# Linear attention, dense gated layer and routed experts on one core: the order of the first loads, of the route's parts and of TensorE around the last route

## The chip, the cores and the metric

The kernel runs on one core of one Trainium2 chip. The metric is the device time of one execution in microseconds (us). A core has TensorE (PE, with its weight loads listed apart as PEld), VectorE (DVE), ScalarE (ACT), GpSimd (POOL) and SyncE (SP), each with an instruction order of its own, which are tied together by semaphores. The order of the instructions on each engine is set when the kernel is built, by a scheduler that starts from the order of the code and from the dependencies that the code states.

## What is computed

Three layers in a row, in float32. Shapes: 8 sequences of 576 tokens, 8 heads of 64; 4608 tokens of 512; a dense gated layer with 1536 hidden channels; 8 experts with 1024 hidden channels.

```python
kv  = einsum('bhsd,bhse->bhde', k, v)                 # per sequence and head
out = einsum('bhsd,bhde->bhse', q, kv)
x   = out / sqrt(mean(out*out, -1) + 1e-6) * g_norm   # -> [4608, 512]
x   = (silu(x @ w_gate) * (x @ w_val)) @ w_out        # dense layer
# experts: only tokens with x @ w_skip > 0; the others are passed through
e   = argmax(x @ w_gate2);  p = softmax(x @ w_gate2)[e]
out = x + p * (relu(x @ w1[e]) @ w2[e])
```

## The kernel before

The tokens are worked on in 12 chunks of 384. Heads come in 4 pairs. For a pair of a sequence, the keys and values lie in DRAM as rows of 5 tokens (1280 numbers, keys then values), 116 rows to a pair (`PK`), and `attn_load` fetches them as 112 and 4 rows into a tile kv (`spread`), and the transposed queries into a tile qt. `attn_unit` does the attention of a pair: `attn_kv` sums keys times values on TensorE (kvp, line 211) and copies the two 64x64 blocks into a block-diagonal matrix kvbd (ScalarE line 213, VectorE line 214); then queries times that matrix (op, line 227), the sum of squares (sq on ScalarE, ms on VectorE, lines 233 to 236), the root on GpSimd (y, line 238), and the normalised tile xn on VectorE (line 240). `make_xT` transposes xn on TensorE (xtps, line 262) and splits it into a high and a low part.

All matrix products of the layers run on numbers that are split into two parts, as three products. The dense layer's weights come as bits of float64 and are brought into this form by the kernel itself: `load_w` fetches 1 MB (raw, line 315), and for each of its two halves ScalarE scales (line 284), VectorE does three steps (cv, cv, raw: lines 286, 287, 290), ScalarE rounds the high part (w, line 296) and GpSimd subtracts (line 254). There are 18 such tiles (12 of the gate and value weights, 6 of the output weights), all converted during chunk 0 and kept afterwards. For each chunk and each f of 12, `moe1_g` does 24 matmuls (gv, line 346), silu on ScalarE, the multiply on VectorE (line 353) and the split of the hidden tile hT, and `moe1_out` does 9 matmuls (acc, line 367) for the f before. The attention of the next chunk is put between them.

When a chunk is done, its rows x are copied out, and during the next chunk VectorE works out 9 logits for each of its tokens (line 400). `chunk_route` then picks the expert (lines 432 to 440), keeps a running count of the tokens per expert (cum, line 443), and lets TensorE rank the tokens (rp, lines 446 and 447); VectorE makes row numbers of that (lines 448 to 452), and GpSimd scatters the rows into one list per expert in DRAM (line 454). After the chunk before the last but one `rank_experts` orders the experts by size, and in the last chunk `early_base` fixes where the first batch ends. The last chunk's logits are done on TensorE instead (`logits_pe`: transposes ltp, line 411, and products lps, line 416), with a route of its own behind it.

The experts are worked on in 9 batches. Batch 0 is the first 256 rows of the largest expert, which are there before the last chunk is routed; it runs around the last chunk's route: `moe2_h` (hp, line 633) and `moe2_out` (yacc, line 721) for each of 8 f. Batch 1 is the rest of that expert and needs the last scatter: its rows xe are loaded by SP (line 601) and transposed on TensorE (xtp, line 618). Batches 2 to 8 are the other experts.

Loads go out on SP's queue in the order of SP's instructions. A load whose tile's buffer is still in use waits on SP, and all behind it with it. Tiles called kv have two buffers, those with the tag w 18.

`after(a, b)` in the code orders instruction a behind b for the scheduler alone, if both are on the same engine; it adds no semaphore.

Of the kernel before, what the change touches and what calls it, by code (L numbers as in the profile page):

```python
# [16 lines left out]
P = 128  # L17
# [12 lines left out]
def attention_moe_moe_kernel(  # L30
# [98 lines left out]
    def attn_qt_load(c, pr):
        if c == 0:  # L130

            t = wp.tile([P, T], F32, tag="w", name="qt0")
        else:
            t = p1.tile([P, T + P], F32, tag="qt", name="qt")
        src = qT_d[pr, :, c * T:(c + 1) * T]
        if c % 3 == 1:
            cut = S - T
            nc.gpsimd.memset(t[:, cut:cut + P], 0.0)
            nc.sync.dma_start(t[:, 0:cut], src[:, 0:cut])
            nc.sync.dma_start(t[:, cut + P:], src[:, cut:])  # L140
        else:
            nc.sync.dma_start(t[:, 0:T], src)
        qt[c, pr] = t

    def attn_load(c, pr):
        if c % 3 != 2:
            b = 2 * (c // 3) + c % 3
# [191 lines left out]
    def moe1_g(c, f):  # L339
# [13 lines left out]
        nc.vector.tensor_tensor(s, ps[1], s, op=ALU.mult)  # L353
# [70 lines left out]
    def chunk_route(c):  # L424
        lg = lgt.pop(c)
        wd = wdesc.rearrange("p (o e) -> p o e", o=1).to_broadcast([P, R, E])
        eb = (elast if c == NCH - 1 else ebase).rearrange("p (o e) -> p o e", o=1).to_broadcast([P, R, E])
# [19 lines left out]
        nc.tensor.matmul(rp, onesb, ca[:, 0:R, :], start=False, stop=True)  # L447
        nc.vector.tensor_tensor(oh, rp, eb, op=ALU.add)
# [176 lines left out]
    def moe2_h(b, f):  # L625
# [142 lines left out]
    for c in range(NCH):  # L768
        for f in range(NF):
# [23 lines left out]
            if c > 0:  # L793
# [39 lines left out]
    chunk_route(NCH - 1)  # L833
    load_xe(1)
# [22 lines left out]
    load_ranks(ORDER[1:])  # L857
    for b, (r, _, n, nt) in enumerate(BATCH):
# [18 lines left out]
        for f in range(NF2):  # L877
# [9 lines left out]
            moe2_h(b, f)  # L887
# [132 lines left out]
```

## Time and profile before

| | before |
|---|---|
| runs, median (lowest to highest of 3) | 1309.68 us (1309.29 to 1310.69) |
| profiled execution, time | 1305.69 us |
| profiled execution, span of its instructions | 1304.0 us |
| busy in the span: PE, PEld | 1266.1 us (97%), 1180.2 us (91%) |
| DVE, ACT, POOL | 639.3 us (49%), 373.5 us (29%), 510.6 us (39%) |
| keys and values, loads of 112 rows | 32 of 560.0 KB |
| weights of the dense layer, loads | 17 of 1024.0 KB, 2 of 512.0 KB |

The profile is of one execution, whose own time stands beside its span. Busy time is the time in which an engine had an instruction under way; a share is that of the whole span, so it is a mean over stages which differ. A pause of TensorE is read from the brackets of its timeline.

### The profile page before, as it was taken

What the parts mean: (1) busy time and instruction counts of PE and PEld (TensorE: products, weight loads), DVE (VectorE), ACT (ScalarE), POOL (GpSimd) and SP (SyncE); (2) the same over time, 40 slices, a digit from 0 to 9 for tenths busy, and PEclk for the clock granted to TensorE, in tenths of its full rate; (3) what the DMA queues carried; (4) which work ended last, traced back from release to release, by engine and by line L of the source; (5) the groups of instructions that cost most, each with busy time, mean ns of one, the idle gap of its engine ahead of it and who ended that gap; (6) DMA issues with size and microseconds to landing.
All of it is one profiled execution on the core that took longest, in us unless ns stands there. A gap on an engine that the chain in (4) does not pass through costs nothing.

```text
span 1304.0 us, 18975 instructions
## 1 busy us (share of the span) xinstructions
PE 1266.1 (97%) x7239; PEld 1180.2 (91%) x7239; DVE 639.3 (49%) x1487; ACT 373.5 (29%) x773; POOL 510.6 (39%) x545
## 2 busy tenths in 40 slices
PE   5998999999999999999999999999999989999997
PEld 5987999999999999999999999999988978899996
DVE  5896817237164371542815418146283243544662
ACT  3664112122121221211212112121122433344441
POOL 4674323233322332223323223223346443566662
PEclk9999999999999999999999999999999999999999
DMA  9663702021120111202102021110121343555631
GB/s 299 234 220 142 229 20 74 25 68 43 39 66 1 44 55 38 73 26 63 37 7 86 8 62 49 31 51 7 51 91 36 131 149 117 170 171 165 218 121 33
DMA packets 43205, 115.68 MB, mean 89 GB/s; under 512 B 8498, under 2 KB 16690, under 8 KB 40928
## 3 DMA queue, kind: packets, MB, share of 16 engines
q1 hardware_dynamic: 31888, 95.78, 22.7%
q0 software_dynamic: 6912, 9.82, 2.2%
q10 hardware_dynamic: 4304, 8.78, 2.1%
q8 instruction: 59, 0.97, 0.3%
q14 instruction: 42, 0.34, 0.1%
HBM read 88.70 MB, written 30.80 MB: 92 GB/s over the span
## 4 chain that ended last, share of the span: by engine, by line
PE 85%; DVE 5%; DMA 4%; POOL 3%; issue 2%; ACT 1%; SPq 0%; DVEq 0%; ACTq 0%; POOLq 0%
PE gv L346 42%; PE acc L367 21%; PE hp L633 7%; PE yacc L721 4%; PE tacc L687 3%; PE kvp L211 3%; PE op L227 2%; DVE dump L400 2%; PE xtps L262 1%; DMA kv<-in_kv_dram 1%; DMA xe<-xs_dram 1%; POOL v L254 1%; DMA raw<-in_w_dram 1%; DVE ex L585 1%; POOL w L254 1%
## 5 line engine op out<-in xcount | busy, mean ns | idle before, releaser
L346 PE MATMUL gv<-xT,w 128*128 128x384 f32 x3456 | 654.7, 339 | 3.8 <-ACT w L296 2.9
L346 PEld LDWEIGHTS gv<-xT,w 128*128 128x128 f32 x3456 | 602.1, 188 | 18.3 <-ACT w L296 4.2
L367 PE MATMUL acc<-w,hT 128*128 128x512 f32 x1296 | 333.3, 397 | 5.0 <-ACT hT L355 4.0
L254 POOL TENSOR_TENSOR hT<-s,hT 128x384 fp32r<-128x384 f32 x144 | 161.6, 1122 | 403.8 <-ACT hT L355 403.3
L367 PEld LDWEIGHTS acc<-w,hT 128*128 128x128 f32 x1296 | 239.3, 188 | 49.3 <-ACT hT L355 5.6
L400 DVE CUSTOM_DVE_ANT_0 dump<-st,w9b 128x512 bf16<-128x512 f32 x297 | 234.4, 789 | 7.0
L353 DVE TENSOR_TENSOR s<-gv,s 128x384 f32<-128x384 f32 x144 | 80.1, 556 | 253.0 <-PE gv L346 186.1
L254 POOL TENSOR_TENSOR v<-rawv,v 128x512 fp32r<-128x512 f32 x102 | 133.6, 1335 | 49.9 <-ACT v L567 49.7
L352 ACT ACTIVATE s<-gv 128x384 f32<-128x384 f32 x144 | 70.6, 490 | 260.4 <-PE gv L346 251.2
L355 ACT ACTIVATE hT<-s 128x384 fp32r<-128x384 f32 x144 | 75.5, 524 | 242.5 <-DVE s L353 241.1
L633 PE MATMUL hp<-xU,v 128*128 128x256 f32 (+7 forms) x768 | 125.8, 308 | 1.6 <-DVE xU L623 1.4
L633 PEld LDWEIGHTS hp<-xU,v 128*128 128x128 f32 x768 | 113.8, 189 | 4.7 <-DVE xU L623 1.7
L238 POOL TENSOR_TENSOR y<-ms,mhalf 128x6 f32<-128x6 f32 x48 | 68.2, 1422 | 109.7 <-DVE ms L236 107.8
L235 DVE TENSOR_REDUCE ms<-sq 128x6 f32<-128x384 f32 x48 | 26.4, 550 | 105.7 <-ACT sq L233 105.7
L567 ACT ACTIVATE v<-rawv 128x512 fp32r<-128x512 f32 x128 | 73.0, 623 | 1.9 <-DMA rawv<-in_v_dram 1.9
L721 PE MATMUL yacc<-v,h2T 128*128 128x512 f32 (+3 forms) x288 | 73.3, 397 | 0.0
L642 DVE SCALAR_TENSOR_TENSOR h2T<-hp,h2T 128x256 fp32r<-128x256 f32 (+7 forms) x64 | 30.5, 479 | 82.3 <-ACT h2T L641 81.1
L721 PEld LDWEIGHTS yacc<-v,h2T 128*128 128x128 f32 (+3 forms) x288 | 50.6, 181 | 11.2
L687 PE MATMUL tacc<-h2T,v 128*128 128x318 f32 (+3 forms) x384 | 58.1, 302 | 2.1 <-ACT h2T L641 2.1
L641 ACT ACTIVATE h2T<-hp 128x256 fp32r<-128x256 f32 (+7 forms) x64 | 27.2, 428 | 104.7 <-PE hp L633 92.1
L254 POOL TENSOR_TENSOR w<-raw,w 128x512 fp32r<-128x512 f32 x34 | 44.7, 1318 | 30.4 <-ACT w L296 29.5
L687 PEld LDWEIGHTS tacc<-h2T,v 128*128 128x128 f32 x384 | 53.8, 189 | 2.9 <-ACT h2T L641 2.8
(131 smaller groups left out, 875.8 us busy)
## 6 DMA issues: line engine op xcount, KB each, us to landing
rawv<-in_v_dram SPq DMA_DIRECT2D x64, 512.0 KB
kv<-in_kv_dram SPq DMA_DIRECT2D x32, 560.0 KB
raw<-in_w_dram SPq DMA_DIRECT2D x17, 1024.0 KB
out_dram<-st SPq DMA_DIRECT2D x36, 256.0 KB
xs_dram<-zrow ACTq DMA_DIRECT2D x8, 781.5 KB
qt<-in_qT_dram SPq DMA_DIRECT2D x32, 192.0 KB
qt<-in_qT_dram SPq DMA_DIRECT2D x32, 96.0 KB
w9b<-in_w_dram ACTq DMA_DIRECT2D x3, 768.0 KB
```

Of the source, the lines that this page charges most:

```text
L238: nc.gpsimd.tensor_tensor(y, ms, mhalf[:, 0:G], op=ALU.pow)
L254: return eng.tensor_tensor(lo, raw, hi.bitcast(F32), op=ALU.subtract)
L346: nc.tensor.matmul(pt, w1t[f][:, wi, i, kk, :], xT[c, kk][:, xi, :], start=(n == 0), stop=(n == 3 * NK - 1))
L352: step["silu"] = nc.scalar.activation(s, ps[0], AF.Silu)
L353: nc.vector.tensor_tensor(s, ps[1], s, op=ALU.mult)
L355: nc.scalar.activation(h[:, 0, :], s, AF.Copy)
L367: nc.tensor.matmul(acc[c, r], hT[c, f][:, hi, r * P:(r + 1) * P], w[:, wi, f % 2, :], start=(f == 0 and n == 0), stop=(f == NF - 1 and n = ...
L400: nc.vector.tensor_tensor_reduce(out=dump, in0=xrow[c, r][:, 0:DM], in1=w9b[m // 3][:, m % 3, :], op0=ALU.mult, op1=ALU.add, scale=1.0, sc ...
L567: after(nc.scalar.activation(w[:, 0, s], raw[:, s], AF.Copy), behind)
L633: nc.tensor.matmul(pt, w[:, wi, kk, cs], xT["m", b, kk][:, xi, :], start=(i == 0), stop=(i == 3 * NK - 1))
L687: nc.tensor.matmul(acc["m", b, d], w[:, wi, f % 2, d * P:(d + 1) * P], h[:, hi, :], start=(f == 0 and n == 0), stop=(f == NF2 - 1 and n == 2),
L721: ins = nc.tensor.matmul(acc["m", b, t][0:q], h[:, hi, t * q:(t + 1) * q], w[:, wi, f % 2, :], start=(f == 0 and n == 0), stop=(f == NF2 - ...
```

## The change

Six things are done.

1. In the start the keys and values and the queries of a pair share a tile (kvq) from the pool of 18 buffers, one for each of the four pairs, so no pair waits for the buffer of another. `attn_load_first` issues the keys and values, and the queries follow in the same tile.
2. Keys and values are loaded as 128 rows (the last 12 belong to the next pair and are not used), by one DMA, in the start and in all later chunks.
3. The order of the code in the start is new: the third pair's load goes ahead of the first weights, and the next chunk's first loads and the second weights are ordered behind named instructions (`behind`).
4. `chunk_route` is cut in two: `route_rows`, with the row numbers and the scatter, is put one f later, and `rank_experts` or `early_base` two f later, each behind the multiply of that f (`step["gv"]`) on VectorE.
5. The load of batch 0's rows goes with `early_base`.
6. In batch 0 the hp matmuls of f = 1, 2, 3 and of f from 4 on are ordered on TensorE behind the second transpose of the last chunk's rows, behind the last lps (f = 2 and 3) and behind rp; the yacc matmuls of f = 0 behind the last lps, later ones behind rp.

The diff, cut to its core:

```diff
+    kv_rows = kv_d.rearrange("b q p s r c -> (b q p) s r c")
+    def attn_kv_load(c, pr, t, behind=None):
+        if c % 3 != 2:
+            b = 2 * (c // 3) + c % 3
+            row = (b * NPR + pr) * PK
+            n = min(P, B * NPR * PK - row)
+            for lo, hi in spread(n):
+                after(nc.sync.dma_start(t[lo:hi], kv_rows[row + lo:row + hi]), behind)
+            kvt[c, pr] = t
...
-    def attn_load(c, pr):
+    def attn_load(c, pr, behind=None):
         if c % 3 != 2:
-            t = p2.tile([P, 2, NR, P], F32, tag="kv", name="kv")
-            for lo, hi in spread(PK):
-                nc.sync.dma_start(t[lo:hi], kv_d[b, pr, lo:hi])
-            kvt[c, pr] = t
-        attn_qt_load(c, pr)
-    attn_load(0, 0)
+            attn_kv_load(c, pr, p2.tile([P, 2, NR, P], F32, tag="kv", name="kv"), behind)
+        attn_qt_load(c, pr, p1.tile([P, T + P], F32, tag="qt", name="qt"), behind)
+    def attn_load_first(pr):
+        t = wp.tile([P, 2 * NR * P + T], F32, tag="w", name="kvq")
+        attn_kv_load(0, pr, t[:, 0:2 * NR * P].rearrange("p (s r c) -> p s r c", s=2, r=NR))
+        return t[:, 2 * NR * P:]
+    attn_qt_load(0, 0, attn_load_first(0))
...
-        nc.vector.tensor_tensor(oh, rp, eb, op=ALU.add)
+        chosen[c] = rp, oh, m1, mk
+    def route_rows(c, behind=None):
+        rp, oh, m1, mk = chosen.pop(c)
+        after(nc.vector.tensor_tensor(oh, rp, eb, op=ALU.add), behind)
...
-    attn_load(0, 1)
+    attn_qt_load(0, 1, attn_load_first(1))
+    qt2 = attn_load_first(2)
     attn_unit(0, 0)
-    for pr in range(1, NPR):
-        if pr + 1 < NPR:
-            attn_load(0, pr + 1)
-        attn_unit(0, pr)
+    attn_unit(0, 1)
     load_w1(0, (step["ms", 0, 0], step["ms", 0, 1]))
+    attn_qt_load(0, 2, qt2)
+    attn_qt_load(0, 3, attn_load_first(3))
+    attn_unit(0, 2)
+    attn_unit(0, 3)
     flush()
...
-    load_w1(1)
+    load_w1(1, (step["ms", 0, 3], step["xn", 0, 3]))
...
-                    attn_load(c + 1, f // 3)
+                    attn_load(c + 1, f // 3, conv_done.get(1) if c == 0 else None)
...
-                if f == -(-(E + 1) * R // lpf):
+                f0 = -(-(E + 1) * R // lpf)
+                if f == f0:
                     chunk_route(c - 1)
+                if f == f0 + 1:
+                    route_rows(c - 1, step["gv"])
+                if f == f0 + 2:
                     if c == NCH - 2:
-                        rank_experts(c - 1)
+                        rank_experts(c - 1, step["gv"])
                     if c == NCH - 1:
-                        early_base()
+                        early_base(step["gv"])
                         load_xe(0)
...
     chunk_route(NCH - 1)
+    route_rows(NCH - 1)
...
+    first_h = (None, step["ltp", 1], step["lps", R - 1], step["lps", R - 1], step["rp"])
+    first_y = (step["lps", R - 1], step["rp"])
...
-            moe2_h(b, f)
+            moe2_h(b, f, first_h[min(f, len(first_h) - 1)] if b == 0 else None)
...
-                        moe2_out(b, f - 1, t)
+                        moe2_out(b, f - 1, t, first_y[min(f, 2) - 1] if b == 0 else None)
```

How this moves instructions is seen in three places. The first is SP's queue at the start of the program, here before (kv and qt0 are a pair's keys with values and its queries, raw the weights as they come, and a name's number tells tiles apart):

```order
L150 DMA kv_88<-in_kv_dram 112x1280
L150 DMA kv_88<-in_kv_dram 4x1280
L142 DMA qt0_91<-in_qT_dram 128x384
L150 DMA kv_166<-in_kv_dram 112x1280
L150 DMA kv_166<-in_kv_dram 4x1280
L142 DMA qt0_169<-in_qT_dram 128x384
L142 DMA qt0_195<-in_qT_dram 128x384
L142 DMA qt0_221<-in_qT_dram 128x384
L315 DMA raw_265<-in_w1_dram 128x2048
L139 DMA qt_377<-in_qT_dram 128x192
L140 DMA qt_377<-in_qT_dram 128x192
L150 DMA kv_192<-in_kv_dram 112x1280
```

and now (kvq holds both):

```order
L134 DMA kvq_88<-in_kv_dram 128x1280
L149 DMA kvq_88<-in_qT_dram 128x384
L134 DMA kvq_164<-in_kv_dram 128x1280
L149 DMA kvq_164<-in_qT_dram 128x384
L134 DMA kvq_167<-in_kv_dram 128x1280
L324 DMA raw_211<-in_w1_dram 128x2048
L149 DMA kvq_167<-in_qT_dram 128x384
L134 DMA kvq_225<-in_kv_dram 128x1280
L149 DMA kvq_225<-in_qT_dram 128x384
L324 DMA raw_302<-in_w1_dram 128x2048
L324 DMA raw_315<-in_w2_dram 128x2048
L324 DMA raw_332<-in_w1_dram 128x2048
```

The third pair stands ahead of the first weights instead of behind them and a load of the next chunk, each pair takes one load for its keys and values, and three more weights follow at once, where before two came and then the next chunk's keys.

The second is TensorE's order at the start of the program, before:

```order
L211 MATMUL kvp_171<-kv_88 128x128 x5
L211 MATMUL kvp_197<-kv_166 128x128 x5
L227 MATMUL op_179<-kvbd00_93,qt0_91 128x128 x3
L227 MATMUL op_205<-kvbd10_97,qt0_169 128x128 x3
L211 MATMUL kvp_223<-kv_192 128x128 x5
L211 MATMUL kvp_244<-kv_218 128x128 x5
L227 MATMUL op_231<-kvbd20_101,qt0_195 128x128 x3
```

and now:

```order
L220 MATMUL kvp_169<-kvq_88 128x128 x5
L220 MATMUL kvp_190<-kvq_164 128x128 x5
L236 MATMUL op_177<-kvbd00_91,kvq_88 128x128 x3
L220 MATMUL kvp_228<-kvq_167 128x128 x5
L236 MATMUL op_198<-kvbd10_95,kvq_164 128x128 x3
L236 MATMUL op_236<-kvbd20_99,kvq_167 128x128 x3
L220 MATMUL kvp_249<-kvq_225 128x128 x5
```

The kvp of the third pair now stands ahead of the op of the second.

The third is TensorE's order around the second part of the last chunk's rank (rp), in batch 0, before:

```order
L633 MATMUL hp<-xU_8842,v_2_8419 128x256 x3
L633 MATMUL hp<-xU_8824,v_3_8522 128x256 x3
L633 MATMUL hp<-xU_8830,v_3_8522 128x256 x3
L446 LDWEIGHTS trib
L446 MATMUL rp<-mk,trib 128x24
L721 MATMUL yacc_9060<-v_2_8471,h2T 128x512 x2
L721 MATMUL yacc_9064<-v_2_8471,h2T 128x512
L721 MATMUL yacc_9060<-v_2_8471,h2T 128x512
L447 LDWEIGHTS onesb
L447 MATMUL rp<-cum_163,onesb 128x24
```

and now:

```order
L651 MATMUL hp<-xU_8801,v_1_8281 128x256 x3
L651 MATMUL hp<-xU_8807,v_1_8281 128x256 x3
L455 LDWEIGHTS trib
L455 MATMUL rp<-mk,trib 128x24
L456 LDWEIGHTS onesb
L456 MATMUL rp<-cum_161,onesb 128x24
L741 MATMUL yacc_9025<-v_0_8229,h2T 128x512 x3
L741 MATMUL yacc_9029<-v_0_8229,h2T 128x512 x3
L651 MATMUL hp<-xU_8789,v_2_8384 128x256
```

Counted from the first transpose of batch 0's rows, 78 hp and 28 yacc matmuls of TensorE's order stood ahead of the second rp, and now 48 and 6.

## Rows read from the trace of the kernel before

**Rows 1.** Timeline, TensorE, first 45 us: start, us, engine, line, operation, [idle before <-releaser]
```profile
6.13 2.50 PE L211 MATMUL kvp<-kv 116*128 116x128 f32 x10 [6.13 <-DMA kv<-in_kv_dram]
...
8.98 2.48 PE L211 MATMUL kvp<-kv 116*128 116x128 f32 x10 [0.36 <-DMA kv<-in_kv_dram]
...
11.26 2.77 PE L227 MATMUL op<-kvbd,qt 128*128 128x128 f32 x12
...
16.21 2.47 PE L211 MATMUL kvp<-kv 116*128 116x128 f32 x10 [2.18 <-DMA kv<-in_kv_dram]
...
28.89 0.88 PE L262 MATMUL xtps<-ident,xn 128*128 128x128 f32 x3 [5.14 <-DVE xn L240]
...
34.31 1.28 PE L211 MATMUL kvp<-kv 116*128 116x128 f32 x10
```

**Rows 2.** Stretches: length, PE, PEld, DVE, ACT, POOL busy (x), clock, DMA share, GB/s
```profile
30.00:40.00 10.00, 10.00 (x61) 9.87 (x60) 9.35 (x16) 6.48 (x13) 5.38 (x6) 0.89 0.63 211
40.00:60.00 20.00, 20.00 (x112) 18.77 (x111) 18.22 (x31) 11.04 (x21) 12.61 (x12) 1.00 0.76 280
60.00:80.00 20.00, 20.00 (x122) 18.77 (x121) 17.30 (x29) 12.45 (x25) 14.99 (x14) 1.00 0.79 253
80.00:100.00 20.00, 17.93 (x91) 15.50 (x90) 18.12 (x29) 12.28 (x22) 13.42 (x11) 1.00 0.48 176
100.00:115.00 15.00, 11.66 (x58) 9.68 (x58) 11.54 (x20) 7.00 (x14) 8.97 (x8) 1.00 0.43 167
```

**Rows 3.** Timeline of the last chunk, TensorE and VectorE
```profile
978.84 0.73 PE L367 MATMUL acc<-w,hT 128*128 128x512 f32 x2 [1.57 <-ACT hT L355]
...
1012.46 0.17 DVE L584 TENSOR_REDUCE gm<-xe 128x2 f32<-128x16 f32 x1 [5.23 <-DMA xe<-xs_dram]
...
1026.63 0.60 PE L618 MATMUL xtp<-ident,xe 128*128 128x128 f32 x4
```

**Rows 4.** Timeline around the last chunk's route, TensorE, VectorE and SyncE
```profile
1036.52 2.99 PE L633 MATMUL hp<-xU,v 128*128 128x256 f32 x23
...
1044.47 1.05 PE L416 MATMUL lps<-w9k,lxt 128*128 128x128 f32 x8
...
1047.70 0.55 DVE L443 TENSOR_TENSOR cum<-cum,mk 128x8 bf16<-128x8 bf16 x3
...
1051.34 0.19 PE L447 MATMUL rp<-cum,onesb 128*128 128x24 bf16 x1
...
1053.12 1.56 PE L721 MATMUL yacc<-v,h2T 128*128 128x512 f32 x6
...
1058.55 1.70 SPq L601 DMA_DIRECT2D xe<-xs_dram  x3
...
1061.29 0.44 PE L618 MATMUL xtp<-ident,xe 128*128 128x128 f32 x2 [2.77 <-DMA xe<-xs_dram]
```

**Rows 5.** Stretches around the wait for xe
```profile
1058.00:1061.00 3.00, 0.52 (x3) 0.09 (x1) 0.00 (x0) 0.00 (x0) 0.00 (x0) 1.00 0.46 120
1061.00:1064.00 3.00, 2.06 (x10) 1.62 (x11) 2.00 (x5) 1.94 (x4) 2.65 (x3) 0.85 0.88 253
1064.00:1067.00 3.00, 3.00 (x18) 3.00 (x17) 1.71 (x9) 0.55 (x3) 0.00 (x0) 0.58 1.00 382
```

**Rows 6.** Timeline of the third batch, TensorE
```profile
1082.87 1.21 PE L633 MATMUL hp<-xU,v 128*128 128x342 f32 x6 [1.38 <-DVE xU L623]
```

**Rows 7.** Stretches of the first 15 us
```profile
0.00:5.00 5.00, 0.00 (x0) 0.00 (x0) 0.46 (x2) 1.49 (x2) 3.55 (x45) 1.00 0.59 148
5.00:10.00 5.00, 3.52 (x15) 3.24 (x16) 0.23 (x1) 0.22 (x1) 0.00 (x0) 1.00 1.03 306
10.00:15.00 5.00, 4.03 (x19) 3.73 (x18) 1.37 (x4) 1.64 (x4) 0.85 (x1) 1.00 1.04 342
```

**Rows 8.** Timeline of the first 45 us, VectorE
```profile
15.06 0.68 DVE L286 TENSOR_SCALAR cv<-raw 128x512 int32<-128x512 int32 x1
...
21.68 0.23 DVE L214 COPY kvbd<-kvp 64x64 f32<-64x64 f32 x1 [1.03 <-ACT kvbd L213]
```

More of the change, by code (lines that the diff above doesn't have):

```diff
@@ L123, in after, with attn_qt_load @@
         return ins
+    kv_rows = kv_d.rearrange("b q p s r c -> (b q p) s r c")
[7 more added lines that the diff above has]
+            kvt[c, pr] = t
     def q_at(c, r):
         return r * P + (P if c % 3 == 1 and r > RS else 0)
[L129 to L134, printed above, removed]
+    def attn_qt_load(c, pr, t, behind=None):
         src = qT_d[pr, :, c * T:(c + 1) * T]
@@ L410, in logits_pe @@
             for kk in range(NK):
-                nc.tensor.transpose(tp[:, kk, :], st[:, kk * P:(kk + 1) * P], ident)
+                step["ltp", r] = nc.tensor.transpose(tp[:, kk, :], st[:, kk * P:(kk + 1) * P], ident)
             xt = [xtp.tile([P, 2, P], F32, tag=f"xn{2 * (r % 2) + i}", name=f"lxt{i}") for i in range(2)]
@@ L415, in logits_pe @@
             for kk in range(NK):
-                nc.tensor.matmul(
+                step["lps", r] = nc.tensor.matmul(
                     lp[:, r, :], xt[kk // 2][:, kk % 2, :], w9[:, kk, :], start=(kk == 0), stop=(kk == NK - 1)
@@ L426, in chunk_route @@
         wd = wdesc.rearrange("p (o e) -> p o e", o=1).to_broadcast([P, R, E])
-        eb = (elast if c == NCH - 1 else ebase).rearrange("p (o e) -> p o e", o=1).to_broadcast([P, R, E])
         for r in range(R):
@@ L446, in chunk_route @@
         nc.tensor.matmul(rp, trib, mk, start=True, stop=False)
-        nc.tensor.matmul(rp, onesb, ca[:, 0:R, :], start=False, stop=True)
-        nc.vector.tensor_tensor(oh, rp, eb, op=ALU.add)
+        step["rp"] = nc.tensor.matmul(rp, onesb, ca[:, 0:R, :], start=False, stop=True)
+        chosen[c] = rp, oh, m1, mk
+    chosen = {}
+    def route_rows(c, behind=None):
+        rp, oh, m1, mk = chosen.pop(c)
+        eb = (elast if c == NCH - 1 else ebase).rearrange("p (o e) -> p o e", o=1).to_broadcast([P, R, E])
+        after(nc.vector.tensor_tensor(oh, rp, eb, op=ALU.add), behind)
         nc.vector.tensor_tensor(oh, oh, mk, op=ALU.mult)
@@ L480, in count, with by_rank @@
         return cp
-    def by_rank(src, name):
+    def by_rank(src, name, behind=None):
         t = xtp.tile([P, E, E], F32, tag="cmp", name="cmp")
-        nc.vector.tensor_tensor(t, sel, over(src, False), op=ALU.mult)
+        after(nc.vector.tensor_tensor(t, sel, over(src, False), op=ALU.mult), behind)
         o = p2.tile([P, E], F32, tag="rk" + name, name="rk" + name)
@@ L488, in by_rank, with rank_experts @@
         return o
-    def rank_experts(c):
+    def rank_experts(c, behind):
         key = p2.tile([P, E], F32, tag="key", name="key")
-        nc.vector.scalar_tensor_tensor(key, count(c), float(2 * E), wdesc, op0=ALU.mult, op1=ALU.add)
+        after(nc.vector.scalar_tensor_tensor(
+            key, count(c), float(2 * E), wdesc, op0=ALU.mult, op1=ALU.add
+        ), behind)
         t = xtp.tile([P, E, E], F32, tag="cmp", name="cmp")
@@ L512, in load_ranks, with early_base @@
             )
-    def early_base():
-        o = by_rank(count(NCH - 2), "o")
+    def early_base(behind):
+        o = by_rank(count(NCH - 2), "o", behind)
         nc.vector.tensor_scalar(adj, o[:, 0:1], -1.0, float(EARLY), op0=ALU.mult, op1=ALU.add)
@@ L623, in make_xT2, with moe2_h @@
         return nc.vector.tensor_tensor(xt[:, 1, :], tpf, xt[:, 0, :].bitcast(F32), op=ALU.subtract)
-    def moe2_h(b, f):
+    def moe2_h(b, f, behind=None):
         r, _, m, nt = BATCH[b]
@@ L632, in moe2_h @@
             for wi, xi in ((0, 0), (0, 1), (1, 0)):
-                nc.tensor.matmul(
+                ins = nc.tensor.matmul(
                     pt, w[:, wi, kk, cs], xT["m", b, kk][:, xi, :], start=(i == 0), stop=(i == 3 * NK - 1)
                 )
+                if i == 0:
+                    after(ins, behind)
                 i += 1
```

9 lines of the change are left out of this document (4 added, 5 removed).

## The prediction

> **What bounds the kernel now.** I read the timeline of TensorE (PE) first and looked in it only for pauses, since a row of it carries the idle time ahead of it in brackets. It falls into four stages. In the first 30 us PE waits: 6.13 us for the first keys and values, 2.18 us for the third pair's, 5.14 us for a normalised tile [rows 1]. Then come the conversions of the weights, up to 115 us: the table by stretches [rows 2] shows PE busy without a pause from 30 to 80 us, and idle for 20.00 - 17.93 = 2.07 and 15.00 - 11.66 = 3.34 us after that, 5.41 in all. In the same rows VectorE (DVE) is busy 9.35 of 10, 18.22 of 20, 17.30 of 20, 18.12 of 20 and 11.54 of 15 us: it bounds this stage, with 85 - 74.53 = 10.47 us not used. From 115 us on the timeline lists no pause above 0.15 us until 1.57 us at 978.84 [rows 3], so the chunks between are PE's own work, and what this change does there can only lose. Last comes the stretch around the last chunk's route: PE stands still 2.77 us for xe, the rows of the first expert that the last scatter completes [rows 4].
>
> That last wait is read as a chain. The last logits matmul (lps) ends at 1044.47 + 1.05 = 1045.52, the route's running sum (cum) on VectorE at 1048.25, but the second rank matmul (rp) runs only at 1051.34, because it stands behind other matmuls in PE's order; 9.95 us later, at 1061.29, PE gets xe [rows 4]. Nothing else of it is long: the chain is started too late.
>
> **The change, part by part.** All sums stand against the profiled execution, 1305.69 us with a span of 1304.00; the runs' median is 3.99 us above it, and I take gains from the median.
>
> *The end.* Ahead of the second rp stood 78 hp, 28 yacc, 12 ltp and 12 lps rows of PE's order; now 48 hp, 6 yacc and the same ltp and lps. So 30 hp and 22 yacc matmuls go behind it. By 2.99 / 23 = 0.130 us for an hp and 1.56 / 6 = 0.26 us for a yacc [rows 4] that is 3.9 + 5.7 = 9.6 us. The route on VectorE must be done by then: it took 1048.25 - 1045.52 = 2.73 us, and between the last lps and rp now lie 6 yacc and 24 hp, 1.56 + 3.12 = 4.68 us of cover. So rp can run at about 1041.7, the same 9.95 us follow (VectorE's index, three scatters of GpSimd, SyncE's load, which was issued at 1058.55 [rows 4] and has the same instructions ahead of it in SP's queue), and xe is there at 1051.7. PE's work ahead of it is the same as before and ends where it did, at about 1058.5. The wait is gone with 6.8 us to spare. What it is worth: PE was busy 0.52 of the 3 us from 1058 and 2.06 of the next 3, so 2.48 + 0.94 = 3.42 us of pauses [rows 5] (2.77 and two short ones that start from a standing PE). In the 6 us from 1061 the granted clock was 0.85 and 0.58 [rows 5], with the fall after the pause: (0.15 + 0.42) x 3 = 1.71 us of PE's work done at the lower level, 1.2 instead of 2.4 GHz. Both go with the wait: 5.13 us. Against it, PE's order now has the last four lps behind a transposed tile that two other engines must copy first, with four lps (0.53 us) in between; bounds are 0 and the 1.57 us that PE once waited for such a hand-over [rows 3], and I take 0.3, near the lower since part is covered. Sum of the end: **4.8 us**, ends 1.85 (3.42 less 1.57, the clock not won) and 6.5 (5.13 and the 1.38 us at 1082.87 [rows 6], where VectorE stood behind a later xe that may now be loaded sooner).
>
> The Trainium skill ("TensorE: Matmul & The Clock Gate", section "What's actually happening") says that the clock's monitor runs free of the kernel, so that whether a pause brings the clock down also depends on when it falls. The one execution shown here has the fall right after this pause; what other runs do it cannot show. By the page the 1.71 us need not go with the pause. That gets a rival of its own.
>
> *The first loads.* The third pair's loads had waited for a buffer until 8.98; now they go out ahead of the first weights, each pair's as one DMA of 128 rows (0.655 MB; 0.594 before). From the bytes by stretches [rows 7]: 0.74 MB had moved by 5 us, then 306 GB/s. The second pair was complete at 1.385 MB, so at 5 + 0.645 / 0.306 = 7.1, and PE began on it at 8.98 [rows 1], 1.9 us later. Three pairs with two qt are 2.36 MB: 10.3, usable at 12.2 instead of 16.21. The first weights end at 3.41 MB, about 15.2. So PE's first 20 us close up. But the stage behind is bound by VectorE, and there the first conversion moves: in VectorE's order it stands behind the second pair's sum of squares, as before, and that now comes later, because PE's order has the third pair's kvp ahead of the second pair's op. Before, op of both ended at 14.03 [rows 1] and the first conversion ran at 15.06 [rows 8], 1.03 us after. Now: 11.46 (kvp 2 ends), one op 1.39 (half of 2.77), kvp 3 2.47, one op 1.39: 16.71, conversion at 17.74, **2.7 us later**. If PE is at its upper level by then (kvp 1.28 as at 34.31 [rows 1]) it is about 0.2 us, bound by the weights at 15.2; if the third pair landed as late as before, at 16.21, it would be 16.21 + 2.47 + 1.39 + 1.03 = 21.10, 6.0 us later.
>
> VectorE has something to pay this back from: the 10.47 us that it did not use, and 1.03 us ahead of its copy at 21.68 [rows 8], which came from a third and fourth pair that were late. Weights two to four now go out ahead of all of the next chunk's keys, where two of them and then a wait for PE came first. On the other hand SP reaches the later waiting loads sooner (the next chunk's last pair with six weights ahead of it, not eight). I take it that the 2.7 us come back and no more: **0 us**, ends a loss of 6.0 and a gain of 5.4, the pauses from 80 to 115 us.
>
> *The route in two parts.* In the chunk before the last the rows' part now comes one multiply later, some 6.3 us. It feeds xe for the first batch, which landed at 1012.46 while the first transpose of it ran at 1026.63 [rows 3]: covered by 14 us; with the cover gone it would be 6.3 us. VectorE's order around 978.84 has one more logit ahead of the multiply that PE waited for and one fewer ahead of the next: 0 us, bounds -1.57 and +1.57 [rows 3], in the middle since the two cancel.
>
> *128 rows in the other chunks.* The 28 later loads carry 0.061 MB more each and are issued once instead of twice. They run a chunk ahead under PE's work, so 0 us; uncovered, 0.061 / 0.306 = 0.2 us each, 5.6 us.
>
> Sum: 4.8 + 0 + 0 + 0 = 4.8 us, and 1309.68 - 4.8 = **1304.9 us**.
>
> **The rivals.** *The start pays too.* PE's pair work closes up, it is at the upper level early, the conversion is 0.2 us late, and a third of VectorE's unused 10.47 us is won: 3.5 - 0.2 = 3.3, so 1301.6. For it: weights two to four early. Against: SP's later waits.
>
> *The start costs.* The 2.7 us are not paid back, since later waits take their place: 1307.6. For it: the stage's end hangs on VectorE, and its unused time lies mostly after 60 us, where buffers and SP's order decide.
>
> *Slower.* The third pair's values share the queue with the first weights and land at 16.2 as before; the first conversion comes 6.0 us late, and PE, standing meanwhile, falls to the lower level once more (1.71 us as above): 1304.9 + 7.7 = 1312.6. It is slower than before from a conversion that is 4.8 us late, thus after 19.9. Against: SP issues these loads without a wait now.
>
> *The clock stays.* The pause goes, but the fall comes anyway at another place of that stretch: 1304.9 + 1.7 = 1306.6.
>
> *The change does not reach the wait.* Something else on SP holds xe's load where it was: 1309.7. Against: SP's order ahead of it is the same.
>
> **How the numbers follow.** Forecast 0.42 (its own range 1302.9 to 1306.9), the start pays 0.22, the start costs 0.18, the clock stays 0.08, slower 0.06, not reached 0.04. A measurement tells about 0.2%, 2.6 us, from no change: the bounds are 1307.1 and 1312.3. Below 1307.1 lie nearly all of the forecast and of "the start pays", most of "the clock stays" and a third of "the start costs": 0.41 + 0.22 + 0.06 + 0.05 = 0.74. Above 1312.3 lies most of "slower": 0.05. The range 1301.0 to 1309.0 takes in the forecast, the clock, nearly all of "the start costs" and two thirds of "the start pays": 0.8.
>
> **What would show it.** Right for the end: no PE pause for xe in the 10 us after the last yacc, rp within 6 us of the last lps, granted clock 1.00 there. Right for the start: the third kvp before 14 us, the first conversion between 15.3 and 18, the last conversion's end within 2 us of where it was, and PE pauses from 30 to 115 us that add up to more than 5.41 by what the first 30 us lose. Wrong: a pause of 2 us or more ahead of rp or lps; a first conversion after 19.9; pauses in the chunks between.

## The result, and the profile after

| | before | after |
|---|---|---|
| runs, median (lowest to highest) | 1310.18 us (1309.29 to 1312.49, 4 runs) | 1295.21 us (1294.35 to 1295.61, 4 runs) |
| ratio of the times, 95% interval | | 0.9882, 0.9865 to 0.9899 |
| profiled execution, time and span | 1305.69 and 1304.0 us | 1295.61 and 1293.9 us |
| PE, PEld busy | 1266.1, 1180.2 us | 1263.8, 1176.7 us |

The change makes the kernel 15.0 us faster by the medians; 4.8 were forecast (1304.9, range 1301.0 to 1309.0). The two profiled executions lie 10.1 us apart. In the rows shown, the lines of the attention and the dense layer stand 9 further down now, those of the experts 18 to 20. Three names of the experts' part come up: xU is the split form of the transposed rows, h2T the split hidden tile, and tacc a product of the second layer in a later batch.

Timeline of the kernel after, TensorE, in the start and by the first pause of the last chunk (start, us, engine, line, operation, idle before and releaser):

```profile
5.36 4.76 PE L220 MATMUL kvp<-kvq 116*128 116x128 f32 x20 [5.36 <-DMA kvq<-in_kv_dram]
...
10.62 1.28 PE L220 MATMUL kvp<-kvq 116*128 116x128 f32 x10
...
14.98 0.91 PE L236 MATMUL op<-kvbd,kvq 128*128 128x128 f32 x6 [2.40 <-DVE ms L245]
...
21.71 2.74 PE L355 MATMUL gv<-xT,w 128*128 128x384 f32 x9
...
972.61 0.73 PE L376 MATMUL acc<-w,hT 128*128 128x512 f32 x2 [1.30 <-ACT hT L364]
```

The first two pairs run without a pause between them. The third pair's kvp is there at 10.62 instead of 16.21, the pause of 5.14 us is gone [rows 1] (the longest behind the first loads is now 2.40 us), and the first gv stands at 21.71 (29.42 before). The pause that stood at 978.84 [rows 3] stands at 972.61: **6.2 us are won ahead of the last chunk's end.**

Stretches of the kernel after, columns as in [rows 2], and the first and last steps of the conversion (VectorE and GpSimd):

```profile
5.00:10.00 5.00, 4.60 (x21) 4.31 (x22) 0.23 (x1) 0.22 (x1) 0.00 (x0) 1.00 1.02 401
10.00:15.00 5.00, 2.60 (x25) 2.44 (x23) 3.02 (x9) 2.54 (x6) 1.37 (x1) 1.00 1.03 418
...
40.00:60.00 20.00, 19.73 (x116) 18.32 (x115) 17.69 (x30) 12.22 (x24) 14.09 (x13) 1.00 0.89 325
60.00:80.00 20.00, 17.22 (x92) 14.78 (x91) 18.92 (x31) 11.98 (x22) 13.32 (x11) 1.00 0.71 285
80.00:100.00 20.00, 19.02 (x98) 16.66 (x97) 18.71 (x30) 12.62 (x23) 13.78 (x12) 1.00 0.46 165
100.00:115.00 15.00, 13.74 (x67) 11.46 (x68) 10.57 (x19) 7.54 (x14) 11.07 (x9) 1.00 0.30 111
```

```profile
13.60 0.68 DVE L295 TENSOR_SCALAR cv<-raw 128x512 int32<-128x512 int32 x1
...
112.26 1.30 POOL L263 TENSOR_TENSOR w<-rawh,w 128x512 fp32r<-128x512 f32 x1 [1.15 <-ACT w L305]
```

Transfers run at 401 and 418 GB/s where they ran at 306 and 342 [rows 7], and the DMA engines are as busy as before (1.02 and 1.03). The last conversion begins at 112.26 instead of 118.34. TensorE's pauses from 30 to 115 us add up to 0.27 + 2.78 + 0.98 + 1.26 = 5.29 us, as before (5.41 [rows 2]): the whole stage has moved forward. The granted clock is not the reason: in the start the lower level took (0.12 + 0.23) x 5 = 1.75 us before (stretches 25:30 and 30:35) and (0.35 + 0.33) x 5 = 3.4 us after (15:20 and 20:25).

The end, timeline of TensorE and VectorE after, and the stretches behind the last of the pauses:

```profile
1028.15 1.95 PE L425 MATMUL lps<-w9k,lxt 128*128 128x128 f32 x16
...
1034.24 0.17 PE L456 MATMUL rp<-cum,onesb 128*128 128x24 bf16 x1
...
1044.14 0.16 DVE L602 TENSOR_REDUCE gm<-xe 128x1 f32<-128x8 f32 x1 [1.63 <-DMA xe<-xs_dram]
...
1047.12 0.38 PE L636 MATMUL xtp<-ident,xe 128*128 128x128 f32 x2
...
1048.78 0.18 DVE L602 TENSOR_REDUCE gm<-xe 114x3 f32<-114x24 f32 x1 [2.31 <-DMA xe<-xs_dram]
...
1049.56 1.65 PE L741 MATMUL yacc<-v,h2T 128*128 128x512 f32 x6 [1.13 <-DVE h2T L662]
...
1070.10 0.18 DVE L602 TENSOR_REDUCE gm<-xe 124x3 f32<-124x24 f32 x1 [5.22 <-DMA xe<-xs_dram]
...
1070.97 1.88 PE L651 MATMUL hp<-xU,v 128*128 128x342 f32 x6 [2.13 <-DVE xU L641]
```

```profile
1070.00:1073.00 3.00, 2.03 (x8) 1.97 (x9) 2.31 (x8) 0.57 (x2) 0.00 (x0) 0.71 0.01 4
1073.00:1076.00 3.00, 3.00 (x17) 2.93 (x16) 0.57 (x2) 0.80 (x2) 1.18 (x2) 0.73 0.14 53
```

rp follows the last lps by 4.1 us (5.8 before [rows 4]), xe is there 9.7 us after rp's end, and TensorE takes it at 1047.12 without a wait. In its place stand two waits for VectorE, 1.13 us, and 2.13 us where 1.38 stood [rows 6], with the clock's fall behind the second. In VectorE's order the gate of a later batch (gm) stands ahead of each and waits for that batch's xe, 2.31 and 5.22 us. From the pause near 975 us to the tacc behind 1140 us that waits 0.24 us it is 167.86 us (172.02 before): **4.2 us are won in the end.** With the 6.2 that is 10.4; behind that tacc 0.3 us are lost, which leaves the 10.1.

### The profile page after: what moved, and what is told of

Read it like the earlier page. It is cut to its first block, busy times and chain, and to the rows that moved or that the text cites. A ratio compares the mean times of both kernels' runs of the same rounds, so it can differ in the third digit from the quotient of the medians.

```text
span 1293.9 us, 18922 instructions
## 1 busy us (share of the span) xinstructions
PE 1263.8 (98%) x7239; PEld 1176.7 (91%) x7239; DVE 639.2 (49%) x1487; ACT 374.7 (29%) x773; POOL 510.8 (39%) x545
## 4 chain that ended last, share of the span: by engine, by line
PE 87%; DVE 5%; DMA 3%; issue 2%; POOL 1%; ACT 1%; SPq 0%; ACTq 0%; POOLq 0%; DVEq 0%
PE gv L355 43%; PE acc L376 22%; PE hp L651 7%; PE yacc L741 4%; PE tacc L707 3%; PE kvp L220 3%; PE op L236 3%; DMA xe<-xs_dram 2%; DVE dump L409 1%; DMA raw<-in_w_dram 1%; PE xtps L271 1%; DVE ex L603 1%; PE xtp L636 1%; DVE cv L296 1%; DVE raw L299 1%
## 5 line engine op out<-in xcount | busy, mean ns | idle before, releaser
L244 DVE TENSOR_REDUCE ms<-sq 128x6 f32<-128x384 f32 x48 | 26.4, 550 | 98.5 <-ACT sq L242 98.4
L758 POOL DMA_INDIRECT out_dram<-y,ids x24 | 27.7, 1153 | 71.5 <-DVE y L755 51.2
```

## The experiments

Every kernel left one profile. The table gives what was read from each: GB/s of the stretches 5:10 and 10:15, starts of the third kvp, the first conversion (cv) and the last (w<-rawh), the first pause near 975 us, the length from there to that tacc ("end"), and the time of that execution, all in us.

| kernel (parts of the change in it) | GB/s | kvp 3 | cv | last w | pause | end | time |
|---|---|---|---|---|---|---|---|
| before | 306, 342 | 16.21 | 15.06 | 118.34 | 978.84 | 172.02 | 1305.69 |
| before_a | 294, 346 | 17.12 | 15.73 | 120.50 | 980.96 | 175.15 | 1311.01 |
| before_b | 296, 343 | 17.05 | 15.03 | 119.47 | 979.98 | 172.29 | 1307.26 |
| end_only (6) | 305, 342 | 16.80 | 14.95 | 119.02 | 979.53 | 168.25 | 1304.28 |
| rows_only (2) | 393, 415 | 14.72 | 13.76 | 113.42 | 973.94 | 174.21 | 1303.39 |
| rows_end (2, 6) | 396, 422 | 14.39 | 13.68 | 113.61 | 974.10 | 168.75 | 1298.04 |
| old_start (2, 4, 5, 6) | 393, 415 | 14.57 | 14.31 | 114.35 | 974.47 | 168.30 | 1297.87 |
| start_only (1 to 5) | 406, 411 | 11.88 | 14.87 | 114.94 | 975.26 | 170.52 | 1300.91 |
| after (all) | 401, 418 | 10.62 | 13.60 | 112.26 | 972.61 | 167.86 | 1295.61 |
| after_again (all) | 395, 418 | 12.02 | 16.35 | 114.81 | 975.10 | 165.33 | 1295.60 |
| after_112 (all, 112 + 4 rows) | 268, 309 | 13.47 | 16.20 | 120.74 | 981.09 | 168.00 | 1305.60 |
| rows_112_16 (all, 112 + 16) | 277, 330 | 13.28 | 17.18 | 122.05 | 982.39 | 166.18 | 1303.66 |
| rows_64_64 (all, 64 + 64) | 254, 306 | 13.65 | 17.89 | 122.97 | 983.32 | 166.27 | 1304.89 |
| gates (all, gates later) | 407, 413 | 11.42 | 14.40 | 114.88 | 975.18 | 163.86 | 1295.40 |
| gates_again (the same) | 391, 416 | 11.95 | 15.03 | 113.75 | 974.09 | 163.52 | 1294.06 |

The first four variants below (end_only, start_only, rows_only, after_112) ran on one chip beside before. The 1295.21 us of the changed kernel is from another group of runs, whose before has the same median; where a variant is compared with it, the difference of the two ratios to before is given too.

**end_only**: the kernel before, with this alone added (and `after` at the matmuls; the rest of it is left out here):

```diff
...
+    first_h = (None, step["ltp", 1], step["lps", R - 1], step["lps", R - 1], step["rp"])
+    first_y = (step["lps", R - 1], step["rp"])
...
-            moe2_h(b, f)
+            moe2_h(b, f, first_h[min(f, len(first_h) - 1)] if b == 0 else None)
...
-                        moe2_out(b, f - 1, t)
+                        moe2_out(b, f - 1, t, first_y[min(f, 2) - 1] if b == 0 else None)
```

> The kernel before with part 6 of the change alone: TensorE's order around the last route. Theory (the end is a chain that started too late; the start has nothing to do with it): rp runs within 6 us of the last lps, xe lands about 9.7 us after rp's end as in the changed kernel, TensorE has no pause for xe there, and the time falls by 4 us, between 3 and 5, so to about 1306 against a median of 1310.2. Rival (the end's gain in the changed kernel came from the route in two parts and the earlier load of batch 0's rows): under 1.5 us. In both, everything up to 1015 us stands as before: the pause of 1.57 us by 978.84 stays where it was, within 1 us.

Measured: 1304.64 us (median of 12 runs, 1302.26 to 1310.03) against 1310.17, ratio 0.9966 (0.9952 to 0.9979), so 2.8 to 6.3 us. The start is as before, the end 168.25. TensorE's timeline of it:

```profile
1037.30 1.95 PE L416 MATMUL lps<-w9k,lxt 128*128 128x128 f32 x16
...
1043.39 0.17 PE L447 MATMUL rp<-cum,onesb 128*128 128x24 bf16 x1
...
1059.29 0.96 PE L723 MATMUL yacc<-v,h2T 128*128 128x512 f32 x3 [1.70 <-DVE h2T L644]
...
1079.77 1.22 PE L633 MATMUL hp<-xU,v 128*128 128x342 f32 x6 [1.20 <-DVE xU L623]
```

rp follows lps by 4.1 us, nothing waits for xe, and the h2T pause is the one that the changed kernel has too: it comes with TensorE's order. The forecast of the chain holds.

**start_only**: the changed kernel with those lines as before (`moe2_h(b, f)`, `moe2_out(b, f - 1, t)`).

> The changed kernel without part 6: hp and yacc are not ordered around the last route. Theory (the start won 6.2 us, which the forecast put at nothing, and the end 4): the time is 4 us above the changed kernel, about 1299, the pause for xe of 2.5 to 3 us is back, and the pause that stood at 978.84 stands at 972.6, within 1 us. Rival (the start's gain was one of that profiled execution alone): the first 115 us are as before, and the time is within 1.5 us of the kernel before less what the two-part route gives.

Measured: 1300.31 us (6 runs, 1298.55 to 1303.75), ratio 0.9933 (0.9916 to 0.9949): 5.1 above the changed kernel by the medians, 6.7 by the ratios, and the pause is back:

```profile
1055.74 0.44 PE L636 MATMUL xtp<-ident,xe 128*128 128x128 f32 x2 [2.93 <-DMA xe<-xs_dram]
```

The pause near 975 us stood at 975.26, outside the stated 1 us: the same start differs by up to 2.7 us between executions. Even so the start is a gain, not chance.

**rows_only**: the kernel before with one load of 128 rows to a pair (`kv_rows` as in the change).

```diff
...
-            for lo, hi in spread(PK):
-                nc.sync.dma_start(t[lo:hi], kv_d[b, pr, lo:hi])
+            row = (b * NPR + pr) * PK
+            for lo, hi in spread(min(P, B * NPR * PK - row)):
+                nc.sync.dma_start(t[lo:hi], kv_rows[row + lo:row + hi])
```

> The kernel before with part 2 alone: 128 rows of keys and values by one DMA, in the tiles and in the order of before. Theory of the rate (keys and values in 112 rows move at 261 to 291 GB/s, as in the stretches 14:19 and 23:28 of before, where weights in 128 rows move at 374 to 382; the first stage was late because of this): the stretches in which keys and values come run at 400 GB/s or more, the third kvp starts 2 to 3 us earlier than 16.21, and 2 to 4 us of the 6.2 are won before 978 us. Rival (order: the third pair's load waited for a buffer, and that is the gain): less than 1 us is won before 978 us, even if the rate rises.

Measured: 1302.91 us (6 runs, 1300.43 to 1304.39), ratio 0.9944 (0.993 to 0.9958), 7.3 below before. The rate rose to 393 and 415, the third kvp came only 1.5 us earlier, yet 4.9 us were won by the pause near 975 us, more than the 2 to 4 that were expected. The rival of the order falls.

**after_112**: the changed kernel with `spread(PK)` again in place of the 128 rows.

> The changed kernel with its keys and values loaded as 112 and 4 rows, as before; tiles and order as changed. Theory of the rate: the first 30 us show 290 to 340 GB/s instead of 339 to 430, the third kvp starts at about 12.5 to 13.5 us instead of 10.62, and of the 6.2 us that the start won 3 to 5 are lost, so 1298 to 1300. Rival (order): at most 1.5 us are lost, so at most 1296.7. Second rival (the rate is a matter of the one execution that was profiled, or of the weights): the stretches of keys and values move at 400 GB/s and more here too.

Measured: 1300.04 us (6 runs, 1299.14 to 1305.6; the profiled one is the slowest), ratio 0.9929 (0.9914 to 0.9945). The rate falls back, the last conversion begins at 120.74, and 4.8 us of the median are lost, 6.2 by the ratios. So the rate is needed for the start's gain in the new order as well. One thing stays open: the median is still 10.1 us below before, and parts 4 to 6 account for some 7.3 of it (below). Whether tiles and order bring the rest while the loads are slow, in the faster executions that were not profiled, isn't shown.

**before_a, before_b**: unchanged.

> The kernel before, unchanged, profiled once more: its runs spread over 6 us, and the profile that the forecast was read from is one of the fastest. Theory (the spread is made in the first 115 us, by when the loads land and in which stretch TensorE falls to its lower level): if this execution is slower than 1305.69, then the pause that stood at 978.84 stands later by nearly all of the difference, and the pause for xe is 2.5 to 3 us as before. Rival (the spread is made at the end): the pause stands at 978.84 within 1 us, and the difference lies behind 1050 us.

> The kernel before, unchanged, profiled a third time. As for the second: by the first theory the place of the pause near 979 us moves with the time of the execution, by the rival it doesn't.

Measured: 1311.01 and 1307.26 us. Neither theory alone: of the 5.3 us by which before_a is slower, 2.1 stand at the pause near 980 us and 3.1 behind it. Its end, TensorE and stretches:

```profile
1063.79 0.69 PE L618 MATMUL xtp<-ident,xe 128*128 128x128 f32 x2 [2.85 <-DMA xe<-xs_dram]
...
1086.60 1.95 PE L633 MATMUL hp<-xU,v 128*128 128x342 f32 x6 [2.26 <-DVE xU L623]
```

```profile
1061.00:1064.00 3.00, 0.21 (x1) 0.21 (x2) 0.20 (x2) 0.00 (x0) 0.20 (x2) 0.81 0.64 158
1064.00:1067.00 3.00, 2.85 (x12) 2.30 (x12) 1.79 (x4) 1.98 (x4) 2.45 (x2) 0.50 0.94 232
1067.00:1070.00 3.00, 3.00 (x17) 3.00 (x16) 1.77 (x10) 0.56 (x3) 0.00 (x0) 0.55 1.01 399
1085.00:1088.00 3.00, 1.40 (x5) 1.40 (x6) 2.17 (x8) 0.57 (x2) 0.00 (x0) 0.80 0.08 33
1088.00:1091.00 3.00, 3.00 (x15) 2.92 (x15) 0.14 (x1) 0.42 (x2) 1.00 (x1) 0.64 0.14 53
```

Summed as for [rows 5], (1 - clock) x 3 us, the lower level took 3.42 us behind the pause for xe and 1.68 behind the next one, 5.1 in all, where the execution that the forecast was read from had 1.71. That execution was also faster than each of the 44 timed runs of before (1306.2 to 1312.68), and this is where the 15.0 by medians and the 10.1 by profiles part. The falls of the clock make a part of it only: in before_b they took 3.42 us, too, and its end is just 0.3 us longer.

**rows_112_16**: the changed kernel with `for lo, hi in ((0, 112), (112, n))`.

> The changed kernel with its 128 rows of keys and values loaded as 112 and 16 rows instead of one DMA of 128. Theory (a DMA of 112 rows is slow in itself): the stretches of keys and values run at 250 to 320 GB/s as with 112 and 4 rows, and the time is that of the run with 112 and 4 rows, 1299 to 1301. Rival (the extra DMA of 4 rows was the slow thing, since it has too few rows for the 16 DMA engines): 390 GB/s and more, and the time is within 1.5 us of the changed kernel's 1295.2.

Measured: 277 and 330 GB/s, 1302.62 us (4 runs, 1298.68 to 1303.66), ratio 0.9949 (0.9933 to 0.9966). The load of 4 rows was not the slow one. The bytes are those of the changed kernel, so the rates compare like with like.

**rows_64_64**: the same with `((0, 64), (64, n))`.

> The changed kernel with its 128 rows loaded as 64 and 64 rows, two DMAs. It tells what makes 112 rows slow. Case one (any DMA of fewer than 128 rows is slow, or two DMAs for one tile are): 250 to 330 GB/s in the stretches 5:10 to 15:20. Case two (112 rows in particular are: 7 rows to each of the 16 DMA engines, where 128 are 8 and 64 are 4): 390 GB/s and more.

Measured, the first stretches beside those of rows_only:

```profile
5.00:10.00 5.00, 2.48 (x10) 2.21 (x10) 0.23 (x1) 0.22 (x1) 0.00 (x0) 1.00 1.05 254
10.00:15.00 5.00, 4.90 (x23) 4.93 (x24) 0.78 (x2) 0.71 (x2) 0.00 (x0) 1.00 0.99 306
```

```profile
5.00:10.00 5.00, 3.96 (x17) 3.67 (x18) 0.23 (x1) 0.22 (x1) 0.00 (x0) 1.00 1.03 393
10.00:15.00 5.00, 3.01 (x19) 2.85 (x19) 2.53 (x7) 2.33 (x5) 1.53 (x2) 1.00 1.02 415
```

Case one: the same bytes in two loads of 64 rows move as slowly as in 112 and 16. One execution, 1304.89 us. Case one has two readings, fewer than 128 rows to a load or two loads to a tile, and no run here tells them apart: no variant fetched a pair by a single load of fewer rows.

**gates**: the changed kernel, with VectorE's gates of batches 2 and 3 ordered behind work that TensorE waits for.

```diff
-        nc.vector.tensor_reduce(m[0:q], lg, axis=AX.X, op=ALU.max)
+        after(nc.vector.tensor_reduce(m[0:q], lg, axis=AX.X, op=ALU.max), behind)
...
-            load_gate(b + 1)
+            load_gate(b + 1, lo)
...
-                load_gate(b + 1)
+                load_gate(b + 1, step["h2"] if b == 2 else None)
```

> The changed kernel with the gates of batches 2 and 3 moved back in VectorE's order: that of batch 2 behind the last xU of batch 1, that of batch 3 behind the second h2T of batch 2. In the changed kernel each stood ahead of work that TensorE waits for, and itself waited for a later xe: 1.13 us at 1049.56 and 2.13 us at 1070.97, with the granted clock at 0.71 and 0.73 in the 6 us behind the second. Theory (these pauses are all that is left of the wait for xe): both pauses go, no granted clock under 1.00 between 1040 and 1100, and 3 to 5 us are won: 1290 to 1292. Rival (another wait takes their place, for v or for xe itself): under 1 us.

Measured: 1294.73 us (4 runs, 1293.18 to 1295.8). Both pauses and the lower clock between 1040 and 1100 are gone, the end is 163.86; but 0.5 us is no gain that can be told. It was timed again, with the changed kernel and a kernel of parts 2 and 6 on the same chip.

**gates_again, after_again**: as gates, and as the change.

> The changed kernel with the gates of batches 2 and 3 moved back, timed once more beside the changed kernel: the first time its end had neither pause nor lower clock and took 2.8 us less from the pause at 975 us on, but that execution had a fall of the clock at 975 us, which the changed kernel's had not, and a new pause of 1.09 us at 1195.60. Theory (the end is 2 to 3 us shorter, the rest was chance): 1.5 to 3 us below the changed kernel on the same chip. Rival (what is saved is lost again behind it): within 1 us of it.

> The changed kernel, unchanged, timed on the same chip as its variants, and profiled once more. Expected: 1294 to 1296.5; the profile shows the last conversion at 112 to 115 us, a pause of 2 to 2.5 us near 1071 to 1074, and behind it the lower granted clock or not, as the execution has it.

Measured: 1294.04 us (1293.78 to 1294.29) and 1294.58 us (1293.92 to 1295.6), 4 runs each. The end is 1.8 us shorter than in after_again, but behind it stands a pause that the changed kernel has not; TensorE, VectorE and GpSimd of gates_again:

```profile
1194.05 0.47 PE L636 MATMUL xtp<-ident,xe 96*128 96x96 f32 x3 [1.09 <-DVE xU L641]
```

```profile
1183.60 0.69 DVE L263 TENSOR_TENSOR v<-rawv,v 128x512 fp32r<-128x512 f32 x1 [0.67 <-ACT v L585]
...
1190.67 2.95 DVE L263 TENSOR_TENSOR v<-rawv,v 128x512 fp32r<-128x512 f32 x1 [0.94 <-ACT v L585]
...
1184.30 8.77 POOL L263 TENSOR_TENSOR v<-rawv,v 128x512 fp32r<-128x512 f32 x7
```

VectorE's piece of v ahead of that xU took 2.95 us, beside GpSimd's. By the medians, 0.5 us apart, the rival holds: what is saved is mostly lost behind. It is the fastest kernel of the study, not by a margin that the runs can tell.

**rows_end**: the edits of rows_only and end_only together, on the kernel before.

> The kernel before with parts 2 and 6 of the change alone: 128 rows by one DMA, and TensorE's order around the last route. Tiles and order of the first loads, the route in two parts and the load of batch 0's rows stay as before. Theory (these two parts are all that the change brings): the time is that of the changed kernel, 1294 to 1297, the last conversion starts at 112 to 115 us, the third kvp stays late (14 to 15 us). Rival (by the times, the kernel with rows alone lies 2.6 us above the changed kernel without part 6, so the tiles and the order of the first loads bring as much): 1297.5 to 1300.

Measured: 1298.04 us (5 runs, 1296.4 to 1298.72) against 1307.98, ratio 0.9914 (0.9896 to 0.9931). By the time the rival; but the pause at 974.10 says that the start lacks nothing, and the end is longer (168.75 against 165.33, neither with a fall of the clock).

**old_start**: the changed kernel with tiles and order of the first loads as before (a `kv` tile and a `qt0` tile to a pair, the loop over pairs as in the kernel before, no `behind`).

> The changed kernel with the tiles and the order of the first loads as before (parts 1 and 3 undone); 128 rows, the route in two parts, the load of batch 0's rows and TensorE's order stay. The kernel with rows and TensorE's order alone took 1298.0 against 1294.6 of the changed kernel on the same chip, and its profile stood level with it at 975 us. Theory (the 3.4 us are the route in two parts and the earlier load; tiles and order of the first loads bring nothing): 1293.5 to 1296, third kvp at 14 to 15 us, the last conversion at 112 to 115 us, and 165 to 168 us from the pause at 975 us to the tacc that waits 0.24 us. Rival (tiles and order of the first loads bring them): 1297 to 1299.

Measured: 1296.57 us (4 runs, 1294.33 to 1297.87) against 1309.14, ratio 0.9902 (0.9884 to 0.9921), between the two. Its profile agrees with the theory at the start (114.35, 974.47). Its end, 168.30, has two falls of the clock:

```profile
975.00:980.00 5.00, 4.11 (x13) 3.28 (x13) 3.57 (x15) 1.36 (x3) 3.21 (x5) 0.66 0.00 0
...
1075.00:1080.00 5.00, 5.00 (x22) 4.45 (x21) 1.03 (x2) 0.91 (x2) 1.19 (x2) 0.70 0.08 32
```

They took (0.34 + 0.30) x 5 = 3.2 us; an estimate without them is 165.1. Whether tiles and order bring a last 1 or 2 us stays open; by the profiles they bring none.

## Why the prediction was wrong

**The end: right.** The chain was started too late, rp stands 4.1 us behind lps (at most 6 was said), xe comes 9.9 us behind the start of rp (9.95 said), and TensorE takes it without a wait. Part 6 is worth 5.5 us in one pair of medians (1310.17 to 1304.64) and 5.1 in the other (1300.31 to 1295.21); 4.8 was forecast. Inside the sum two terms were off, in opposite directions, so that the sum came out this close is partly luck. The new wait, put at 0.3, is anything from none (rows_112_16) to 1.70 us (end_only) and sits elsewhere: not at lps but at h2T, behind a gate on VectorE that waits for the xe of batch 2. The clock, put at 1.71 from one execution, took 1.71, 5.10 and 3.42 us in the three profiles of before; after, 1.68 in one and nothing in the other.

**The first loads: wrong, and this is the step that failed.** The forecast put them at 0 us; 128 rows in place of 112 and 4 brought 4.8 to 7.3. "From the bytes by stretches [rows 7]: ... then 306 GB/s" was taken as the rate of the queue, and the 128 rows were costed as "0.061 MB more each". The rate was that of the loads of 112 rows. The trace of before shows it where they run nearly alone, in stretches that the forecast did not use:

```profile
14.00:19.00 5.00, 2.58 (x12) 2.32 (x11) 4.14 (x10) 2.50 (x5) 3.33 (x3) 1.00 1.02 291
23.00:28.00 5.00, 0.75 (x7) 0.51 (x6) 4.97 (x11) 3.17 (x7) 2.72 (x3) 1.00 1.05 261
```

In 9:14, with a MB of weights in 128 rows among them, it was 374. Part 2, put at nothing, is worth 7.3 us alone (1310.17 to 1302.91) and 4.8 in the changed kernel (1300.04 against 1295.21). An estimate from these rows: SP issues ten pairs of keys and values in the first 80 us; 10 x 0.594 MB at 0.27 are 22.0 us of transfer, 10 x 0.655 at 0.41 are 16.0. Between them lie 6.0 us. The last conversion came forward by 6.1 in the two profiles of before and after (118.34 to 112.26) and by 5.3 in the mean of all (119.33 over the four with the start of before, 114.00 over the eight with 128 rows). From the first conversion to the last it takes 103.3 to 105.1 us in all seven profiles with fewer rows, and 98.5 to 100.5 in all eight with 128, whatever the order. That loads bounded a part of this stage shows in ScalarE's waits for the weights up to 125 us (total, times, longest), here of before, rows_only and after:

```profile
ACT raw L284 <- DMA raw<-in_w_dram: 14.6, 7, 3.1
...
ACT raw L286 <- DMA raw<-in_w_dram: 6.0, 5, 2.6
...
ACT raw L293 <- DMA raw<-in_w_dram: 5.1, 4, 1.8
```

VectorE's 10.47 unused us [rows 2] lie behind that: its own waits in before, 7.0 us from 30 to 115, name ScalarE, TensorE and GpSimd. The forecast's "it bounds this stage" read VectorE's busy share as a bound. In after_112 these waits of ScalarE are 6.6 us, so there most of the loss lies elsewhere; 2.5 us are TensorE's waits for the next chunk's queries.

The Trainium skill says for most bandwidth to use 128 partitions and at least 1 MiB to a DMA ("DMA: Bandwidth & Descriptors", section "Rules for kernel authors"). The traces agree on the partitions: 401 and 418 GB/s against 254 to 346, with 0.655 MB to a DMA.

**The order in the start.** With slow loads (after_112, rows_112_16, rows_64_64) the chain of the forecast comes out nearly as it was worked: first conversion at 16.20, 17.18 and 17.89 (17.74 said), third kvp at 13.28 to 13.65 (before 14 said). The last conversion begins 1.4 to 3.6 us behind the mean of before's four starts (119.33), so that "the 2.7 us come back" is not what these profiles show; those of after_112 and rows_112_16 are of the slowest execution of each. With 128 rows the first conversion begins at 13.60 to 16.35, and the order costs and brings nothing by the pause near 975 us (972.61 to 975.26 with the new order, 973.94 to 974.47 with the old). Of the forecast's signs for the start one came in the first profile after, the third kvp before 14 us; the first conversion (13.60) came too early, the last conversion's end moved by 6.1 us, and the pauses from 30 to 115 us did not grow. A slip that reached no term of the sum: 3.41 MB at the forecast's 306 GB/s end at 13.7 us, not at 15.2.

**The route in two parts** was put at 0 with bounds of 1.57. From the pause near 975 us to the last lps it takes 57.37 us in rows_end and 55.53 in after_again: 1.8 us for parts 4 and 5, outside the bound (in old_start and gates a fall of the clock at the start of this stretch hides it). 1.1 of it is won in the first 17 us, where two pauses of 0.60 and 0.41 became one of 0.22: the two changes of VectorE's order did not cancel. What brings the other 0.7 stays open.

**128 rows in the other chunks:** 0, as said; from the last conversion's end to the pause near 975 us it is 859.2 before and 859.1 after.

Of the rivals, "the start pays too" named the right side, with 3.3 us where parts 1 to 5 bring 9.9 (1310.17 to 1300.31), and a wrong cause. "The clock stays" holds for one execution of two: in the first profile after, the fall stands behind the next pause. The same pause of before was followed by 1.71, 3.42 and 3.42 us. The Trainium skill says that the window in which the clock's monitor counts runs free and does not start over with the kernel ("TensorE: Matmul & The Clock Gate", section "What's actually happening"), and the three values agree with that. The baseline was the last fault: one profiled execution, faster than all timed runs, gave the end its price of the clock.

## What to carry to other kernels

Read the rate of a queue in stretches where one kind of load runs alone, at each shape, before a load's cost is worked out from bytes; loads that fill all 128 partitions in one DMA may be worth more than a better order of them, even with bytes that nobody needs. Where an engine is busy 90% and another waits for it, look once more at what it waits for itself. And price a fall of the clock from several executions, not from the one profile at hand.

## What the runs showed of the hardware that was not expected

- The rate of loads depends on how the rows are cut into DMAs, at nearly equal busy share of the DMA engines (1.02 to 1.05): 254 GB/s (64 + 64 rows), 268 (112 + 4), 277 (112 + 16), 391 to 407 (128) in the stretch 5:10.
- At the start the matmuls take twice as long, as at the lower level, while the granted clock's column shows 1.00: ten kvp took 2.50 us at 6.13 and 1.28 at 34.31 [rows 1]. In the changed kernel the short time is there from 10.62 on (1.28).
- Like pauses do and don't bring the clock down: behind 1.75, 1.84 and 2.13 us it fell (rows_112_16, old_start, after), behind 2.37 and 2.46 it did not (start_only, rows_end).
- The same step of VectorE, v<-rawv,v, took 0.69 us at 1183.60 and 2.95 at 1190.67, towards the end of a run of that step on GpSimd (gates_again). Beside such a run in after_again it took 1.37 and 1.25, so the overlap alone doesn't set the time.
